# A bias prologue that stores its last blocks in two steps and divides the network's pieces anew

## The chip, the core and the metric

The kernel runs on one core of a Trainium2 chip. The metric is the device time of one execution in microseconds (us), and of several executions the median. The engines are named as the profile names them: PE (TensorE, matrix products; PEld is its weight load), DVE (VectorE), ACT (ScalarE), POOL (GpSimd) and SP (SyncE, which only issues DMA transfers here; ACT and POOL have queues for issuing them too).

## What is computed

Attention over 8 batches, 8 heads, 576 positions and head size 64, with a position bias that a small network makes, and behind it a gated network of three matrix products on all 4608 tokens:

```python
scores = scale * np.matmul(q, k.transpose(0, 1, 3, 2))
psi_rel = np.log1p(np.abs(pos[:, None] - pos[None, :]))
psi_i = np.log1p(np.maximum(pos[:, None], 1.0))
h = np.maximum((psi_rel / psi_i)[..., None] @ w1 + b1, 0.0)   # 32 hidden values per pair (i, j)
scores = scores + (h @ w2).transpose(2, 0, 1)[None]           # one bias per head, the same for every batch
attn = softmax(scores)
x = (attn @ v) with the heads side by side                    # 4608 x 512
out = ((x @ moe_w1) * (x @ moe_w2)) @ moe_w3 @ moe_w_out
```

The bias depends on the head and on the pair of positions (i, j) alone: for a row i it is a function of the distance |i - j|, scaled by a factor of the row. So it is computed once, ahead of the attention, and kept in DRAM.

## The kernel before, in words

**The prologue** (inside `with ExitStack() as pro`) makes the bias in 36 groups of 16 rows. A group has four *pieces* of the network: `hidden(grp)` computes relu of one piece for all distances that the group needs (304 to 576 columns), on DVE (`zdve`, 14 buffers, L534) or on ACT (`zact`, 6 buffers, L532). `bias_group(G)` then multiplies the four pieces by `w2` on PE into a `bacc` bank in PSUM (L549, four banks), and ACT evicts it twice, once forwards and once mirrored, into a tile `bev` of 128 partitions by 591 columns (L562). Partition 8 i + h of `bev` is row i of the group for head h. SP stores the tile into `nb_d` in DRAM (L564, 295.5 KB). The tile comes from the pool `ep`, which has four buffers, so the eviction of group G waits until the store of group G - 4 has landed. Which pieces ACT takes is chosen by a small planner with costs per column (`COST`, `who`).

**Loading the bias.** The attention works on units (p, b): a pair of heads p and a batch b, 32 units. For each unit nine tiles of scores are made: tiles 0 to 7 (rows 128 (t // 2) onwards of head t % 2 of the pair) and M (the last 64 rows of both heads). `load_bias(0, t, True)` fetches the bias tile `nb` of the first pair from `nb_d` (L270, L272, L273, on SP) when its last group is stored: tiles 6 and 7 need group 31, tile M group 35. The first unit needs heads 0 and 1 alone; the other six heads are wanted when the next pairs of heads begin, from unit 6 on.

**Units.** For a unit, S (L320, PE) makes scores of a tile, T (L331, DVE) adds the bias and takes the row's extreme, E (L356, ACT) makes the exponentials, F (L377 to L389, PE) transposes them, H (L400 on DVE, L402 on ACT) moves these out of PSUM into `PTX[u % 2]`, W (L434, PE) multiplies by `v`. `ORDER` gives each step a time within the unit; units follow each other every `PERIOD` = 12.31. The order of T is 0, 3, 1, 5, 6, 2, 7, M, 4. Ahead of S stand the splits of `k` and `q` into a high and a low part: for unit 0 on ACT (L300) and DVE (L301), for every later unit on POOL (gk and gq, L303 and L304). `raw` has one buffer for `k` and one for `q`, so the next unit's load (L287, SP) waits for the split of the one before. `ppM` tiles have zeros at their sides, which POOL clears after the prologue (L589).

**Order of the work.** Each step is put into a list with a due time (`put`, `plan.append`), and `drive` issues a list in the order of these times. There are separate lists for the prologue (all that is due before 0) and for the attention (`later`). DVE, ACT, PE and POOL keep to the order within a list, but a step of a later list may be put among those of an earlier one; SP's order is chosen by the framework. An engine runs its instructions in order, so one that waits holds all behind it. Group G is due at -48 + 1.25 G, with its pieces 0.7 before that, its products 1.0 and its eviction 2.5 after it.

**Memory.** The prologue's pools lie on a stack, in the order in which they are opened, and `ppool` (the exponentials), `pt` (the two `PTX` tiles) and `sm` take their place afterwards.

Of the kernel before, what the change touches and what calls it, by code (L numbers as in the profile page):

```python
# [9 lines left out]
F32 = mybir.dt.float32  # L10
# [7 lines left out]

P = 128

LEAD, PACE_B, BUSY_D, BUSY_A, LAG_B = 48.00, 1.25, 1.95, 4.50, 6.15

FIRST = {"ldk": -42.0, "ldq": -41.0, "ldv": -4.0, "gk": -20.0, "gq": -15.0}
AT_LOW = -4.80
AT_BIAS = -0.7, 1.0, 2.5

AT_FO, PACE_F = 2.00, 2.80
# [71 lines left out]
def relpos_attention_moe(  # L99
# [17 lines left out]
    nc = tc.nc  # L117
    NPAIR, B, _, S = k.shape
    D, H = P // 2, 2 * NPAIR
# [90 lines left out]
    def drive(plan):  # L210

        E_ = mybir.EngineType
        with tc.manual_schedule(engines={E_.PE, E_.Activation, E_.DVE, E_.Pool}):
            for _, _, step in sorted(plan, key=lambda e: e[:2]):
                step()

    def put(plan, steps, *times):

        def one():
            next(steps, None)  # L220
        for at in times:
            plan.append((at, len(plan), one))
# [8 lines left out]
    NB_L, NB_W = 16, S + 32  # L231
    nb_d = dram.tile([H, (S + 1) * NB_W], F32, name="nb_d")
# [17 lines left out]
    st = {u: {"P": [None] * 9} for u in range(NU)}  # L250
# [10 lines left out]
    def load_bias(p, t, first=False):  # L261
        nb = NB[p, t] if first else nbp.tile([P, S], F32, name="nb")
        NB[p, t] = nb
        heads = (0, 1) if t == "M" else (int(t) % 2,)
        for h in heads:
            o = nb[(lo, hi)[h]] if t == "M" else nb
            r0 = 512 if t == "M" else int(t) // 2 * P
            rows = nb_v[2 * p + h, r0:r0 + o.shape[0], :]
            if h == 0:
                nc.sync.dma_start(o, rows)  # L270
            else:
                nc.sync.dma_start(o[:, S - 512:S], rows[:, 0:512])  # L272
                nc.sync.dma_start(o[:, 0:S - 512], rows[:, 512:S])  # L273
# [185 lines left out]
    later = []  # L459
# [7 lines left out]
        later.append((at, len(later), step, n, u))  # L467
    t_s = max(e[0] for e in later if e[3][0] in "SE") + 0.5
    end = max(e[0] for e in later) + 0.5
    later = [e[:3] for e in later]  # L470

    plan = [e for e in later if e[0] < 0.0] + [(AT_LOW, len(later) + i, lambda n=n: st[0].pop("low" + n)()) for i, n in enumerate("kq")]
    later = [e for e in later if e[0] >= 0.0]


    with ExitStack() as pro:
        sb = pro.enter_context(tc.tile_pool(name="pro", bufs=1))
        zp = pro.enter_context(tc.tile_pool(name="zp", bufs=14))
        ep = pro.enter_context(tc.tile_pool(name="ep", bufs=4))
        psb = pro.enter_context(tc.tile_pool(name="psb", bufs=4, space=PSUM))  # L480

        GI = P // HID
        NG = S // GI
        GM = GI * H
        GV = P // GM
        NGRP = NG // GV
        GR = GV * GI

        w1c = sb.tile([P, 1], F32, name="w1c")
        b1c = sb.tile([P, 1], F32, name="b1c")
        w2b = sb.tile([P, GM], F32, name="w2b")
        tsh = sb.tile([P, S], F32, name="tsh")
        beta = sb.tile([P, NG], F32, name="beta")
        post = sb.tile([P, NGRP], F32, name="post")
        nc.scalar.dma_start(w1c, w1.rearrange("g c -> (g c)").rearrange("(p o) -> p o", o=1))
        nc.sync.dma_start(tsh, logs.broadcast_to([P, S]))
        nc.scalar.dma_start(b1c, b1.rearrange("(p o) -> p o", o=1))
        nc.sync.dma_start(beta, logi)  # L500
        nc.scalar.dma_start(w2b, w2)
        nc.sync.dma_start(post, ilogs)
        nc.vector.tensor_scalar(beta, beta, b1c, None, op0=ALU.mult)
        nc.vector.tensor_scalar(tsh, tsh, w1c, None, op0=ALU.mult)

        def reach(G):

            return (G + 1) * GR - 1, S - 1 - G * GR


        COST = {"dve": (0.06, 0.00066), "act": (0.2, 0.00081)}
        busy = dict(dve=BUSY_D, act=BUSY_A)
        who = {}

        def charge(e, n):
            busy[e] += COST[e][0] + COST[e][1] * n

        for G in range(NGRP):
            n = max(reach(G)) + 1
            for vv in range(GV):  # L520
                e = min(busy, key=lambda e: busy[e] + COST[e][0] + COST[e][1] * n)
                who[G * GV + vv] = e
                charge(e, n)
            for m in (reach(G)[1] + 1, reach(G)[0]):
                charge("act", m)

        def hidden(grp):
            n = max(reach(grp // GV)) + 1
            on = who[grp]
            z = zp.tile([P, S], F32, name=f"z{on}", bufs={"dve": 14, "act": 6}[on])  # L530
            if on == "act":
                nc.scalar.activation(z[:, 0:n], tsh[:, 0:n], AF.Relu, bias=beta[:, grp:grp + 1])  # L532
            else:
                nc.vector.tensor_scalar(  # L534
                    z[:, 0:n], tsh[:, 0:n], beta[:, grp:grp + 1], 0.0, op0=ALU.add, op1=ALU.max,
                )
            return z

        def bias_group(G):
            L, R = reach(G)  # L540
            n = max(L, R) + 1
            zs = [hidden(g) for g in range(G * GV, (G + 1) * GV)]
            yield
            accs = []
            for c in range(0, n, 512):
                m = min(n - c, 512)
                acc = psb.tile([P, 512], F32, name="bacc")
                for vv in range(GV):
                    nc.tensor.matmul(  # L549
                        acc[vv * GM:(vv + 1) * GM, 0:m], w2b, zs[vv][:, c:c + m], start=True, stop=True,  # L550
                    )
                accs.append(acc)
            yield

            ev = ep.tile([P, S + GR - 1], F32, name="bev")
            for c, acc in zip((0, 512), accs):
                for at, d, a, b in ((L, 1, 0, R + 1), (L, -1, 1, L + 1)):
                    a, b = max(a, c), min(b, c + 512)
                    if a < b:
                        o = ev[:, at + a:at + b] if d > 0 else ev[:, at - b + 1:at - a + 1]  # L560
                        x = acc[:, a - c:b - c]
                        nc.scalar.activation(o, x if d > 0 else x[:, ::-1], AF.Copy, scale=post[:, G:G + 1])  # L562
            r0 = G * GR * NB_W + 1
            nc.sync.dma_start(  # L564
                nb_d[:, r0:r0 + GR * (NB_W + 1)].rearrange("h (i w) -> i h w", i=GR)[:, :, 0:L + R + 1], ev,
            )


        for G in range(NGRP):
            at = -LEAD + G * PACE_B  # L570
            put(plan, bias_group(G), *(at + d for d in AT_BIAS))
            for t in TILES:
                if G == (NGRP - 1 if t == "M" else 8 * (int(t) // 2) + 7):
                    plan.append((at + AT_BIAS[-1] + LAG_B, len(plan), lambda t=t: load_bias(0, t, True)))
        drive(plan)


# [14 lines left out]
    later = [e for e in later if e[0] >= t_s]  # L592
# [251 lines left out]
    for i in range(2 * NF):  # L844
        at = t_o + i * PACE_F
        hf, t = divmod(i, NF)
# [7 lines left out]
    later = [e for e in later if e[0] > end]  # L854
# [4 lines left out]
    plan, t_f = [], t_o + 2 * NF * PACE_F  # L859
# [22 lines left out]
    for i in range(len(EARLY_W), 2 * NF):  # L882
        n, k = divmod(i - len(EARLY_W) + 1, len(FREE_W))
# [103 lines left out]
```

## Time and profile before

| what | us |
|---|---|
| median of three runs (lowest, highest) | 1103.02 (1101.92, 1104.57) |
| the profiled execution's own time | 1102.86 |
| its span, from the first instruction to the last | 1101.0 |
| PE, DVE, ACT, POOL busy | 1062.7, 846.4, 679.1, 283.8 |
| first eviction of the prologue begins, last one ends | 9.28, 61.44 |

A row of the timeline or of a group names the engine, the line of the kernel, the operation, and output and input by the program's names; in square brackets is the idle time of the engine just before and what ended it. "x4" is a count. In the chain of waits each piece is a start, a length and what it is. SPq rows are issues of DMA transfers, which aren't counted as work of an engine.

### The profile page before, as it was taken

What the parts mean: (1) busy time and instruction counts of PE and PEld (TensorE: products, weight loads), DVE (VectorE), ACT (ScalarE), POOL (GpSimd) and SP (SyncE); (2) the same over time, 40 slices, a digit from 0 to 9 for tenths busy, and PEclk for the clock granted to TensorE, in tenths of its full rate; (3) what the DMA queues carried; (4) which work ended last, traced back from release to release, by engine and by line L of the source; (5) the groups of instructions that cost most, each with busy time, mean ns of one, the idle gap of its engine ahead of it and who ended that gap; (6) DMA issues with size and microseconds to landing.
All of it is one profiled execution on the core that took longest, in us unless ns stands there. A gap on an engine that the chain in (4) does not pass through costs nothing.

```text
span 1101.0 us, 23555 instructions
## 1 busy us (share of the span) xinstructions
PE 1062.7 (97%) x9300; PEld 889.2 (81%) x9300; DVE 846.4 (77%) x1746; ACT 679.1 (62%) x1288; POOL 283.8 (26%) x214
## 2 busy tenths in 40 slices
PE   6769999999999999999999999999999999999998
PEld 3257777777777777767898899999999999999997
DVE  8948887888788888867777867776786786777664
ACT  6869998898898899854433543453453445346332
POOL 0046774776677567530000000000000000000000
PEclk9979999999999999999999999999999999999999
DMA  6974575558455655327322131031012103101001
GB/s 215 284 226 126 175 216 172 157 176 270 131 168 172 201 160 175 98 68 173 115 82 86 44 115 58 1 115 34 24 51 79 44 1 115 29 1 58 1 1 58
DMA packets 58157, 123.19 MB, mean 112 GB/s; under 512 B 9152, under 2 KB 19264, under 8 KB 58048
## 3 DMA queue, kind: packets, MB, share of 16 engines
q1 hardware_dynamic: 56464, 119.95, 34.7%
q10 hardware_dynamic: 1584, 1.75, 0.5%
q8 instruction: 73, 1.20, 0.5%
q14 instruction: 36, 0.29, 0.1%
HBM read 91.76 MB, written 29.92 MB: 111 GB/s over the span
## 4 chain that ended last, share of the span: by engine, by line
PE 82%; DVE 8%; ACT 5%; DMA 3%; issue 1%; ACTq 0%; SPq 0%; DVEq 0%
PE up L767 27%; PE o L823 15%; PE pst L434 14%; PE s L320 13%; PE pst L377 6%; PE wacc L652 4%; DMA nb_d<-bev 2%; PE bacc L549 1%; ACT bev L562 1%; DVE url L737 1%; DVE wmag L193 1%; DVE wu L204 1%; ACT pt L402 1%; DVE g L785 1%; ACT gh L791 1%
## 5 line engine op out<-in xcount | busy, mean ns | idle before, releaser
L331 DVE CUSTOM_DVE_ANT_0 ts<-s,nb 128x576 f32<-128x576 f32 x288 | 211.1, 756 | 59.8 <-PE s L320 26.4
L356 ACT ACTIVATE pp<-ts,mx 128x576 f32<-128x576 f32 x256 | 195.3, 766 | 17.8 <-DVE mx L331 17.8
L767 PE MATMUL up<-xch,urh 128*128 128x384 f32 x560 | 189.8, 339 | 0.0
L767 PE MATMUL up<-xcl,urh 128*128 128x384 f32 x560 | 189.5, 338 | 0.0
L767 PE MATMUL up<-xch,url 128*128 128x384 f32 x560 | 189.0, 337 | 0.0
L823 PE MATMUL o<-w3s,gh 128*128 128x512 f32 x576 | 180.6, 395 | 0.0
L434 PE MATMUL pst<-pt,rv 128*64 128x320 f32 (+1 forms) x1280 | 169.3, 411 | 1.3 <-ACT pt L402 1.3
L791 ACT ACTIVATE gh<-g 128x384 fp32r<-128x384 f32 x96 | 50.5, 526 | 174.7 <-DVE g L785 174.7
L402 ACT ACTIVATE pt<-pst 128x1024 f32<-128x1024 f32 x128 | 128.6, 1020 | 30.7 <-PE pst L377 30.5
L785 DVE TENSOR_TENSOR wos<-up,wos 128x384 f32<-128x384 f32 x120 | 66.9, 558 | 99.4 <-PE up L767 98.3
L434 PEld LDWEIGHTS pst<-pt,rv 128*64 128x64 f32 x1280 | 86.3, 137 | 62.4 <-issue 10.1
L782 ACT COPY wos<-up 128x384 f32<-128x384 f32 x136 | 65.0, 478 | 114.9 <-PE up L767 113.3
L320 PE MATMUL s<-kh,qh 64*128 64x288 f32 x640 | 116.7, 357 | 8.7 <-DVE mx L331 7.7
L823 PE MATMUL o<-w3s,gl 128*128 128x512 f32 x288 | 113.9, 396 | 0.0
L767 PEld LDWEIGHTS up<-xch,urh 128*128 128x128 f32 x560 | 105.3, 188 | 9.2
L767 PEld LDWEIGHTS up<-xch,url 128*128 128x128 f32 x560 | 105.2, 188 | 9.1
L823 PEld LDWEIGHTS o<-w3s,gh 128*128 128x128 f32 x576 | 105.3, 188 | 5.5
L377 PE MATMUL pst<-ident,pp 64*128 64x64 f32 x2304 | 103.2, 225 | 2.3 <-ACT pp L356 1.3
L767 PEld LDWEIGHTS up<-xcl,urh 128*128 128x128 f32 x560 | 105.1, 188 | 0.0
L377 PEld LDWEIGHTS pst<-ident,pp 64*128 64x128 f32 x2304 | 99.9, 140 | 5.2 <-ACT pt L402 2.3
L400 DVE COPY pt<-pst 64x64 f32<-64x64 f32 (+3 forms) x160 | 82.1, 514 | 26.0 <-PE pst L434 24.2
L320 PE MATMUL s<-kh,ql 64*128 64x288 f32 x640 | 97.3, 295 | 0.0
(107 smaller groups left out, 1985.7 us busy)
## 6 DMA issues: line engine op xcount, KB each, us to landing
rq<-in_q_dram SPq DMA_DIRECT2D x31, 640.0 KB
wi<-in_moe_w_dram SPq DMA_DIRECT2D x32, 512.0 KB
nb_d<-bev SPq DMA_DIRECT2D x36, 295.5 KB
rv<-in_v_dram SPq DMA_DIRECT2D x32, 320.0 KB
x_d<-pt SPq DMA_DIRECT2D x32, 288.0 KB
xr<-x_d SPq DMA_DIRECT2D x24, 384.0 KB
rk<-in_k_dram SPq DMA_DIRECT2D x31, 288.0 KB
rb<-r_d SPq DMA_DIRECT2D x44, 192.0 KB
```

The costliest lines, as they stand in the source:

```text
L320: nc.tensor.matmul(s[:, hf, :HS], Q[x][rows, q0:q0 + P], K[y][rows, h * HS:(h + 1) * HS], start=(m == 0), stop=(m == len(ops) - 1),)
L331: nc.vector.tensor_tensor_reduce(out=halves(ts), in0=d.pop(("s", t))[:, :, :HS], in1=halves(NB[p, t]), op0=ALU.add, op1=ALU.min, scale=-1. ...
L356: nc.scalar.activation(pp, ts, AF.Exp, bias=mx, scale=-1.0, accum_out=sums[p][:, 9 * b + col:9 * b + col + 1])
L377: nc.tensor.transpose(ps[0:n, hf, c0:c0 + 64], x[rows], ident[rows, rows])
L400: nc.vector.tensor_copy(o, x)
L402: nc.scalar.activation(o, x, AF.Copy)
L434: nc.tensor.matmul(o, x[:, c0:c0 + D], m, start=(c == 0), stop=(c == 4))
L767: nc.tensor.matmul(acc, l[:, b, ks], r[:, k], start=(m == 0 and which in ("P1", "P2", "P5")), stop=(m == 3 * KH - 1), skip_group_check=whi ...
L782: nc.scalar.copy(d[name], d[src])
L785: nc.vector.tensor_tensor(o, a, b, op=op)
L791: nc.scalar.activation(d["gh"][:, i * CH:(i + 1) * CH], d["g"][:, i], AF.Copy)
L823: nc.tensor.matmul(d["o", t], l[:, sl], folded[ft][r], start=(ft == 0 and m == 0), stop=(ft == NF - 1 and m == 2),)
```

## The change

The last eight groups (`LATE_G` = 28 and up) store in two steps. SP first stores heads 0 and 1 alone, in two transfers of 16 partitions each; when the prologue's list reaches `AT_REST`, POOL's queue stores the whole tile, heads 0 and 1 again among it. These groups have a pool of their own, `eq`, with eight buffers; the other groups' pool `ep` has five in place of four, and is opened ahead of `zp`. The loads of bias tiles 6, 7 and M are due 3.00 after the last eviction that they need, in place of 6.15. The planner is replaced by a rule: ACT takes two pieces in each of groups 0 to 2, one in two groups of three from 3 to 27, none from 28 on. The POOL splits of unit 1 (gk and gq) go into the prologue's list, where they stand ahead of the whole stores.

```diff
--- before.py
+++ after.py
@@ -18,10 +18,11 @@
 P = 128
-LEAD, PACE_B, BUSY_D, BUSY_A, LAG_B = 48.00, 1.25, 1.95, 4.50, 6.15
+LEAD, PACE_B, LAG_B, LAG_L = 48.00, 1.25, 6.15, 3.00
 FIRST = {"ldk": -42.0, "ldq": -41.0, "ldv": -4.0, "gk": -20.0, "gq": -15.0}
 AT_LOW = -4.80
+LATE_G, AT_REST = 28, 6.00
 AT_BIAS = -0.7, 1.0, 2.5
 AT_FO, PACE_F = 2.00, 2.80
@@ -467,16 +468,17 @@
         later.append((at, len(later), step, n, u))
     t_s = max(e[0] for e in later if e[3][0] in "SE") + 0.5
     end = max(e[0] for e in later) + 0.5
-    later = [e[:3] for e in later]
-    plan = [e for e in later if e[0] < 0.0] + [(AT_LOW, len(later) + i, lambda n=n: st[0].pop("low" + n)()) for i, n in enumerate("kq")]
-    later = [e for e in later if e[0] >= 0.0]
+    first = [("gk", 1), ("gq", 1)]
+    plan = [e[:3] for e in later if e[0] < 0.0 or e[3:] in first] + [(AT_LOW, len(later) + i, lambda n=n: st[0].pop("low" + n)()) for i, n in enumerate("kq")]
+    later = [e[:3] for e in later if e[0] >= 0.0 and e[3:] not in first]
     with ExitStack() as pro:
         sb = pro.enter_context(tc.tile_pool(name="pro", bufs=1))
+        ep = pro.enter_context(tc.tile_pool(name="ep", bufs=5))
         zp = pro.enter_context(tc.tile_pool(name="zp", bufs=14))
-        ep = pro.enter_context(tc.tile_pool(name="ep", bufs=4))
+        eq = pro.enter_context(tc.tile_pool(name="eq", bufs=8))
         psb = pro.enter_context(tc.tile_pool(name="psb", bufs=4, space=PSUM))
         GI = P // HID
@@ -508,25 +510,13 @@
             return (G + 1) * GR - 1, S - 1 - G * GR
-        COST = {"dve": (0.06, 0.00066), "act": (0.2, 0.00081)}
-        busy = dict(dve=BUSY_D, act=BUSY_A)
-        who = {}
-        def charge(e, n):
-            busy[e] += COST[e][0] + COST[e][1] * n
-        for G in range(NGRP):
-            n = max(reach(G)) + 1
-            for vv in range(GV):
-                e = min(busy, key=lambda e: busy[e] + COST[e][0] + COST[e][1] * n)
-                who[G * GV + vv] = e
-                charge(e, n)
-            for m in (reach(G)[1] + 1, reach(G)[0]):
-                charge("act", m)
+        def on_act(G):
+            return 2 if G < 3 else 0 if G >= LATE_G else int(G % 3 < 2)
         def hidden(grp):
             n = max(reach(grp // GV)) + 1
-            on = who[grp]
+            on = "act" if grp % GV < on_act(grp // GV) else "dve"
             z = zp.tile([P, S], F32, name=f"z{on}", bufs={"dve": 14, "act": 6}[on])
             if on == "act":
                 nc.scalar.activation(z[:, 0:n], tsh[:, 0:n], AF.Relu, bias=beta[:, grp:grp + 1])
@@ -552,7 +542,7 @@
                 accs.append(acc)
             yield
-            ev = ep.tile([P, S + GR - 1], F32, name="bev")
+            ev = (ep if G < LATE_G else eq).tile([P, S + GR - 1], F32, name="bev")
             for c, acc in zip((0, 512), accs):
                 for at, d, a, b in ((L, 1, 0, R + 1), (L, -1, 1, L + 1)):
                     a, b = max(a, c), min(b, c + 512)
@@ -561,17 +551,22 @@
                         x = acc[:, a - c:b - c]
                         nc.scalar.activation(o, x if d > 0 else x[:, ::-1], AF.Copy, scale=post[:, G:G + 1])
             r0 = G * GR * NB_W + 1
-            nc.sync.dma_start(
-                nb_d[:, r0:r0 + GR * (NB_W + 1)].rearrange("h (i w) -> i h w", i=GR)[:, :, 0:L + R + 1], ev,
-            )
+            o = nb_d[:, r0:r0 + GR * (NB_W + 1)].rearrange("h (i w) -> i h w", i=GR)[:, :, 0:L + R + 1]
+            if G < LATE_G:
+                nc.sync.dma_start(o, ev)
+            else:
+                for h in range(2):
+                    nc.sync.dma_start(o[:, h], ev[h:P:H])
+                yield
+                nc.gpsimd.dma_start(o, ev)
         for G in range(NGRP):
             at = -LEAD + G * PACE_B
-            put(plan, bias_group(G), *(at + d for d in AT_BIAS))
+            put(plan, bias_group(G), *(at + d for d in AT_BIAS), *((AT_REST + 0.1 * G,) if G >= LATE_G else ()))
             for t in TILES:
                 if G == (NGRP - 1 if t == "M" else 8 * (int(t) // 2) + 7):
-                    plan.append((at + AT_BIAS[-1] + LAG_B, len(plan), lambda t=t: load_bias(0, t, True)))
+                    plan.append((at + AT_BIAS[-1] + (LAG_B if G < LATE_G else LAG_L), len(plan), lambda t=t: load_bias(0, t, True)))
         drive(plan)
```

## The prediction

> **What bounds the kernel now.** I began with the table of windows, to see from where on TensorE never waits.
>
> ```profile
> core 0: us, PE busy (x) PEld busy (x) DVE busy (x) ACT busy (x) POOL busy (x), PEclk, DMA share, GB/s
> 9.28:61.45 52.17, 40.14 (x369) 15.92 (x361) 46.64 (x128) 42.62 (x99) 2.09 (x2) 1.00 0.84 263
> 49.70:61.45 11.75, 9.80 (x104) 4.31 (x104) 8.29 (x18) 9.49 (x24) 2.09 (x2) 1.00 0.96 301
> 61.45:67.80 6.35, 0.64 (x6) 0.41 (x6) 0.82 (x3) 1.64 (x5) 4.27 (x6) 0.62 0.77 249
> 86.30:98.85 12.55, 12.55 (x189) 9.64 (x186) 10.21 (x28) 11.62 (x24) 8.38 (x8) 1.00 0.45 138
> 111.40:460.00 348.60, 347.57 (x5010) 265.43 (x5007) 290.83 (x725) 310.34 (x628) 237.12 (x171) 1.00 0.56 176
> ```
>
> Columns: stretch, its length, then busy time and count of PE, PEld, DVE, ACT and POOL, then granted clock, DMA share, GB/s. From 86.30 on PE is busy 12.55 of 12.55 us, later 347.57 of 348.60: whatever moves PE's work at 86.30 moves the end by as much. Ahead of it PE does nearly nothing from 61.45 to 67.80 (0.64 of 6.35), and then runs at a lower clock (0.62 here). In the bias prologue (9.28 to 61.45) ACT is the fullest after DVE, 42.62 of 52.17, and at its end the DMA engines are full: 0.96, 301 GB/s. So next, the chain of waits around the hole, and the table of waits up to 100 us.
>
> ```profile
> 34.32 3.18 DMA nb_d<-bev
> 48.13 4.52 DMA nb_d<-bev
> 61.46 0.52 SPq L564
> 62.07 0.54 SPq L270
> 62.66 4.81 DMA nb<-nb_d
> 67.80 2.53 PE s L320 x18
> ```
>
> ```profile
> ACT bev L562 <- DMA nb_d<-bev: 6.2, 9, 1.6
> DVE ts L331 <- DMA nb<-nb_d: 5.6, 1, 5.6
> ```
>
> The last store goes out, SP then issues the loads of bias tiles 6 and 7, and T6, the fifth softmax step of unit 0, waits 5.6 us for them. Before that ACT lost 6.2 us in nine waits for one of the four `bev` buffers, each behind a store of 3.2 to 4.5 us (3.18 and 4.52 above). The timeline gives the instants:
>
> ```profile
> 9.28 0.85 ACT L562 ACTIVATE bev<-bacc,post 128x512 f32<-128x512 f32 x2 [3.07 <-PE bacc L549]
> 5.47 24.74 DVE L534 TENSOR_SCALAR zdve<-tsh,beta 128x576 f32<-128x576 f32 x70
> 54.18 0.90 ACT L562 ACTIVATE bev<-bacc,post 128x80 f32<-128x80 f32 x2
> 60.38 1.06 ACT L562 ACTIVATE bev<-bacc,post 128x16 f32<-128x16 f32 x3 [1.56 <-DMA nb_d<-bev]
> 55.11 0.53 SPq L564 DMA_DIRECT2D nb_d<-bev  x1
> 52.86 0.75 DVE L301 TENSOR_TENSOR kl<-rk,kh 128x576 fp32r<-128x576 f32 x1
> 53.53 1.49 DVE L301 TENSOR_TENSOR ql<-rq,qh 128x1280 fp32r<-128x1280 f32 x1
> 55.94 0.76 DVE L331 CUSTOM_DVE_ANT_0 ts<-s,nb 128x576 f32<-128x576 f32 x1 [0.93 <-PE s L320]
> 66.98 0.76 DVE L331 CUSTOM_DVE_ANT_0 ts<-s,nb 128x576 f32<-128x576 f32 x1 [5.61 <-DMA nb<-nb_d]
> ```
>
> Group 31's eviction (the 128x80 row) ends at 55.08 and its store is issued at 55.11; the last eviction, group 35, waits 1.56 us for a buffer and ends at 61.44. DVE finishes its pieces of the network at 52.86, then splits `k` and `q` (to 55.02). T0 starts at 55.94, T6 at 66.98.
>
> **The change part by part.** *Pieces of the network.* The prices:
>
> ```profile
> L331 DVE CUSTOM_DVE_ANT_0 ts<-s,nb 128x576 f32<-128x576 f32 x288 | 211.1, 756 | 59.8 <-PE s L320 26.4
> L562 ACT ACTIVATE bev<-bacc,post 128x512 f32<-128x512 f32 (+34 forms) x80 | 33.1, 495 | 12.6 <-DMA nb_d<-bev 6.2 <-PE bacc L549 6.2
> L532 ACT ACTIVATE zact<-tsh,beta 128x496 f32<-128x496 f32 (+13 forms) x17 | 11.7, 689 | 0.0
> L534 DVE TENSOR_SCALAR zdve<-tsh,beta 128x576 f32<-128x576 f32 (+17 forms) x126 | 45.4, 449 | 2.1 <-PE bacc L549 2.0
> ```
>
> ACT goes from 18 to 23 pieces of 144, by the old planner's arithmetic against the new rule: 6 in groups 0 to 2 (before 1), 17 in groups 3 to 27 (before 12), none from 28 on (before 5). DVE gets 121 instead of 126. Its pieces cost 45.4/126 = 0.36 us each; five long early ones and five of middle length leave it and five long late ones come, so 43.5 in place of 45.4: from 5.47 they end at 49.0 if never held, and at 51 if the 2 us of holds of now (52.86 - 5.47 - 45.4) stay. I take 50.2; the splits (2.16) end at 52.4, T0 follows at 52.9, and T6, four steps of 0.76 us and some waits for TensorE later, could run at 56.7. The six early pieces on ACT end at 5.47 + 6 x 0.69 = 9.6, where its first eviction started at 9.28: 0.3 late, since it idled there.
>
> *Five buffers, then eight of their own.* From its first eviction ACT needs 42.6 us of work; its later pieces are as many (17) and a little shorter (-1). With no wait for buffers it ends group 35 at 9.6 + 41.6 = 51.3, and group 31 four evictions (about 4 us) earlier, at 47.3; with half of the 9.5 us of waits of now, at 52. I take 48.5 for group 31.
>
> *Two heads first.* Eight stores of 295.5 KB are replaced on SP by 16 of an eighth of that, 37 KB each.
>
> ```profile
> L564 SPq DMA_DIRECT2D nb_d<-bev x36: 517/524/1228, 10.4 to 61.5; - x36
> ```
>
> SP pays 0.52 us an issue, so 1.04 a group, about ACT's own pace: nothing lies behind it but loads. In the critical stretch 8 x 295.5 - 16 x 36.9 = 1774 KB (1.8 MB) are gone, 6 us of full DMA at 301 GB/s. No row shows the landing of a store this small: between 2 us (half of the quickest whole store) and 4.52; I take 4, since whole stores of groups 23 to 27 stand in the same queues. By the Trainium skill (DMA: Bandwidth & Descriptors, Anatomy of one DMA — SWDGE path) a DMA costs about 2.0 us and its bytes at 436 GB/s, an estimate of 2.1 us here, by which T6 could be up to 1.9 us earlier; its rule (Rules for kernel authors) that transfers under 64 KB are mostly overhead speaks against cutting a store in pieces. No row here shows either. The loads of tiles 6 and 7 then go out at 48.5 + 1.0 + 4 = 53.5 and land after 0.54 + 4 (now 0.54 + 4.3): 58. So T6 starts at 56.7 to 58, I take 57.3: 9.7 us earlier. Bounds 55 and 60.
>
> *Next late: GpSimd.* Here lies the price of the change.
>
> ```profile
> 45.79 0.40 PE L320 MATMUL s<-kh,qh 64*128 64x288 f32 x2 [0.76 <-ACT qh L300]
> 84.72 1.91 ACT L402 ACTIVATE pt<-pst 128x1024 f32<-128x1024 f32 x2
> 63.85 1.26 POOL L303 TENSOR_SCALAR qh<-rq 128x1280 fp32r<-128x1280 f32 x1 [1.95 <-DMA rq<-in_q_dram]
> 65.19 2.89 POOL L304 TENSOR_TENSOR ql<-rq,qh 128x1280 fp32r<-128x1280 f32 x1
> 71.87 0.67 POOL L303 TENSOR_SCALAR kh<-rk 128x576 fp32r<-128x576 f32 x1 [3.79 <-PE s L320]
> 75.35 2.92 POOL L304 TENSOR_TENSOR ql<-rq,qh 128x1280 fp32r<-128x1280 f32 x1
> 61.49 0.41 POOL L589 MEMSET ppM<- 128x64 f32 x4 [1.08 <-ACT bev L562]
> 72.62 0.59 PE L320 MATMUL s<-kh,qh 64*128 64x288 f32 x2
> 57.32 0.54 SPq L287 DMA_DIRECT2D rq<-in_q_dram  x1
> 86.30 0.38 PE L320 MATMUL s<-kh,qh 64*128 64x288 f32 x2
> ```
>
> Unit 1's `q` is loaded once the split of unit 0's has freed its buffer (issue 57.32, use 63.85, 6.5 us), and GpSimd's last piece of unit 1 ends at 68.08, 4.5 us ahead of S0 of unit 1 (72.62). Now the split ends at 52.4, the load goes out at 53.5 and takes 5.2 with fewer stores beside it, and gq of unit 1 ends after 4.3 us more at 63.0: S0 of unit 1, due at 72.62 - 9.7 = 62.9, just gets it. Putting gk and gq of unit 1 into the prologue's plan keeps them ahead of the stores. But the eight whole stores stand next on GpSimd. They overwrite what tiles 6, 7 and M read, so they wait for these loads (58, and some 60 for M, hidden behind gq, which ends at 63). Behind them stand gk and gq of unit 2, 71.87 to 78.27, so 6.4 us, possibly the four clears of `ppM` (0.4 us), and then S0 of unit 2, which is at 86.30 now with 8 us of slack.
>
> No DMA is issued by GpSimd in this trace. A store there costs no less than SP's 0.52 us, and at most GpSimd's longest instruction, 2.92. I take 1.2, the nearest row that isn't SP's quick case: the longest issue of this very store on SP (1.228). By the Trainium skill (same page, SWDGE vs HWDGE vs iDMA and the latency table) the path from GpSimd has a program write its descriptors and takes about 1 us to the first byte; with 1.0 the sum below gives 1094.2.
>
> Unit 2's `q` is then ready at 63.0 + 8 x 1.2 + 0.4 + 6.4 = 79.4, needed 0.2 us after S0's start. S0 of unit 2 stands at 79.2, 7.1 us earlier than 86.30. With 0.52 GpSimd is done at 74.0 and the 9.7 us of T6 hold; with 2.92 it is done at 93.2 and the kernel loses 6.7. The break-even is (86.5 - 69.8)/8 = 2.1 us a store.
>
> *Without price.* `eq` lies behind `zp`, so under the second `PTX` tile, whose first write is H0 of unit 1 (84.72 now, 77 then); the last store is issued at 72.6 and has left `eq` by 77. If that cover fails ACT waits by the lateness. The stores' bytes move to where DMA has room (0.77 from 61.45, 0.45 from 86.30).
>
> **Sum.** The profiled execution took 1102.86 us (span 1101.0 and 1.86 around it); 1102.86 - 7.1 = 1095.8. The median of the runs, 1103.02, differs by 0.16 only, so 1095.8 it is.
>
> **Rivals.**
> *A. GpSimd doesn't decide* (a store costs under 0.9 us, or gk of unit 2 is put ahead of the stores): all of T6's 9.7 us arrive, and, PE's clock being kept, about 1 us more (S0 of unit 2 stands 19.3 us after T6 now, 18.35 in the order as written): 1092 to 1093. For it: ready instructions overtake here (S0's first product runs at 45.79 among the bias products). Against: the stores are ready when gq ends.
> *B. The load is late anyway.* DMA is full: groups 3 to 27 come faster (one whole store per 1.2 us of ACT is 250 GB/s, and `k`, `q` and six bias tiles beside them, 2.7 MB in 34 us, make it 330, over the 301 of the fullest stretch), so a backlog stands ahead of the small stores. Each us of it beyond my 4 lands on T6; with 5 us T6 gains 4.7 and the time is 1098. Against: 6 us of DMA are taken out, and five stores may be on their way.
> *C. Slower.* A store on GpSimd costs over 2.1 us: S0 of unit 2 is later than 86.5 and PE waits in order; at 2.5 us it is 3.3 us late, 1106. For it: POOL's 128-partition operations take 1.26 to 2.92 us. Against: a store touches no data on GpSimd. The Trainium skill (SBUF — State Buffer, Who interferes with whom) says that DVE in its two-port mode keeps GpSimd from writing descriptors; the pieces of the network are such instructions, but they are over 10 us before the stores, so by it C gets no more.
> *D. No change:* the store costs 2.1, or order changes eat the gain. 1102.5.
>
> **Numbers.** Forecast 0.55, A 0.15, B 0.14, C 0.11, D 0.05. The forecast's own range, stores of 1.0 to 1.6 us, is 1094 to 1099; the range that holds the time 8 times in 10 takes in most of A and B, 1091 to 1100.5. What this measurement tells from no change is 0.2%, 2.2 us. Faster: forecast, A and nearly all of B, 0.83; same: D and a rest of B, 0.06; slower: C, 0.11.
>
> **What would show it.** In the profile after: ACT's waits for `bev` buffers under 2 us; evictions over by 54; T6 at 55 to 60 with a wait for `nb` under 2 us; GpSimd's eight stores between 60 and 75, about 1.2 us apart; S0 of unit 2 near 79, held by `ql`; PE full from there. The prediction is wrong if T6 comes after 61, if the stores cost under 0.9 or over 1.8 us each, or if S0 of unit 2 waits for something else.

## The result, and the profile after

The changed kernel is slower: 1114.78 us (median of four runs, 1113.53 to 1115.66) against 1103.23 (1101.92 to 1104.57), a ratio of 1.0114 with a 95% interval of 1.01 to 1.0128. The forecast was 1095.8 with a range to 1100.5: wrong in sign.

The profiled execution of after took 1115.66 us, span 1113.8: 12.8 more than that of before. First the sums of its page: did any engine get more work?

```profile
PE 1061.1 (95%) x9300; PEld 887.0 (80%) x9300; DVE 844.9 (76%) x1741; ACT 681.0 (61%) x1293; POOL 288.7 (26%) x222
```

None did: PE is busy for 1061.1 us, 1.6 less than before. So a gap must have opened, and the table of windows of TensorE shows it (stretch, length, PE's busy time and count, granted clock, DMA share, GB/s):

```profile
50.00:55.00 5.00, 4.42 (x45) 1.00 0.33 103
...
70.00:75.00 5.00, 0.67 (x6) 0.68 0.99 320
75.00:80.00 5.00, 2.23 (x16) 0.50 0.97 363
80.00:85.00 5.00, 0.00 (x0) 0.50 0.44 153
```

From 70 to 85 us PE works 2.90 of 15 us, and what it does then runs at 0.50 to 0.68 of the clock. The timeline of VectorE (T0, T6, tile M's step and, behind the gap, a step of unit 1), ScalarE, GpSimd and PE:

```profile
49.73 3.48 DVE L524 TENSOR_SCALAR zdve<-tsh,beta 128x560 f32<-128x560 f32 x8
54.34 1.06 ACT L552 ACTIVATE bev<-bacc,post 128x16 f32<-128x16 f32 x3 [0.66 <-PE bacc L539]
55.90 0.76 DVE L332 CUSTOM_DVE_ANT_0 ts<-s,nb 128x576 f32<-128x576 f32 x1 [0.63 <-PE s L321]
...
64.28 0.76 DVE L332 CUSTOM_DVE_ANT_0 ts<-s,nb 128x576 f32<-128x576 f32 x1 [5.40 <-DMA nb<-nb_d]
...
73.42 0.76 DVE L332 CUSTOM_DVE_ANT_0 ts<-s,nb 128x576 f32<-128x576 f32 x1 [6.33 <-DMA nb<-nb_d]
...
73.70 2.14 POOL L561 DMA_DIRECT2D nb_d<-bev  x4 [2.64 <-DMA nb<-nb_d]
...
82.86 1.94 ACT L403 ACTIVATE pt<-pst 128x1024 f32<-128x1024 f32 x2 [14.63 <-issue]
85.58 0.76 DVE L332 CUSTOM_DVE_ANT_0 ts<-s,nb 128x576 f32<-128x576 f32 x1 [9.24 <-ACT pp L357]
...
97.15 0.38 PE L321 MATMUL s<-kh,qh 64*128 64x288 f32 x2
```

And the view of line 561, the whole stores:

```profile
L561 POOL DMA_DIRECT2D nb_d<-bev x8: 530/532/714, 66.0 to 75.3; - x8
...
who waited for it (us, times):
  ACT pt L403: 14.6, 1
...
DMA to landing us min/median/max: 3.6/6.6/8.8
```

The 82.86 row is H0 of unit 0, the first write into `PTX`. ACT was free at 68.23 and sat idle for 14.63 us. The row itself names no releaser ("issue" stands for time in which the profile shows none); the view of the stores does: what waited for them is "ACT pt L403", 14.6 us. ACT runs in order, so the exponentials behind H0 stand too, and with them T (9.24 us at 85.58, "ACT pp") and S. The 97.15 row is 10.85 us later than its counterpart in before (86.30). The prediction calls that row S0 of unit 2, but it is S3, the step behind it: a unit has ten such rows (one for each tile, two for M), and this is the 22nd. S0 itself went from 84.75 to 95.61, so the delay is the same. How much of it arrives at the end shows in the store of a unit's result, `x_d`, whose first and last issue stand in one row of that tensor's view. Before:

```profile
L443 SPq DMA_DIRECT2D x_d<-pt x32: 319/327/1267, 95.8 to 498.3; - x32
```

After:

```profile
L444 SPq DMA_DIRECT2D x_d<-pt x32: 319/327/538, 106.6 to 511.0; - x32
```

The first unit is done 10.8 us later (106.6 against 95.8), the last 12.7 (511.0 against 498.3), the span is 12.8 longer. So most of the loss is in the start, and 1.9 us more are lost between the first unit and the last.

### The profile page after: what moved, and what is told of

It reads as the page before. It is cut to its first block, busy times and chain, and to the rows that moved or that the text cites. A ratio compares the mean times of both kernels' runs of the same rounds, so it can differ in the third digit from the quotient of the medians.

```text
span 1113.8 us, 23596 instructions
## 1 busy us (share of the span) xinstructions
PE 1061.1 (95%) x9300; PEld 887.0 (80%) x9300; DVE 844.9 (76%) x1741; ACT 681.0 (61%) x1293; POOL 288.7 (26%) x222
## 4 chain that ended last, share of the span: by engine, by line
PE 80%; DVE 9%; ACT 6%; issue 3%; DMA 2%; SPq 0%; POOL 0%; ACTq 0%; DVEq 0%; POOLq 0%
PE up L762 27%; PE o L818 15%; PE pst L435 14%; PE s L321 12%; PE pst L378 6%; PE wacc L647 4%; DMA nb_d<-bev 1%; ACT bev L552 1%; DVE wmag L194 1%; ACT pp L357 1%; DVE url L732 1%; ACT pt L403 1%; DVE wu L205 1%; ACT zact L522 1%; DVE zdve L524 1%
## 5 line engine op out<-in xcount | busy, mean ns | idle before, releaser
L403 ACT ACTIVATE pt<-pst 128x1024 f32<-128x1024 f32 x128 | 128.6, 1021 | 44.5 <-PE pst L378 29.7
```

What stands on the lines that cost most here:

```text
L403: nc.scalar.activation(o, x, AF.Copy)
```

## The experiments

The theory: H0 waits not for what lies under the tile that it writes but for what lies under the whole pool `pt`, from which both `PTX` tiles come. `eq` lies under the second tile only (by the program's allocation it takes bytes 122784 to 141724 of a partition; the first tile is 99520 to 122560, the second 122560 to 145600), so the prediction let only H0 of unit 1 wait. The rivals: the two steps of storing cost the time in another way (queues, DMA traffic), or the new division does.

### Two pools for PTX

```diff
-    pt = att.enter_context(tc.tile_pool(name="pt", bufs=1))
+    pt = [att.enter_context(tc.tile_pool(name=f"pt{i}", bufs=1)) for i in range(2)]
...
-    PTX = [pt.tile([P, 9, SQW], F32, name=f"pt{i}") for i in range(2)]
+    PTX = [pt[i].tile([P, 9, SQW], F32, name=f"pt{i}") for i in range(2)]
```

> The changed kernel, but the two PTX tiles come from two pools in place of one; they keep their places in memory, and eq lies under the second alone. Theory (the first H step of unit 0 waits for GpSimd's whole stores because the pool of both PTX tiles opens as one over eq): that wait of 14.6 us goes, H0 of unit 0 starts within 1 us of its transposes (near 70), and the time falls by 9 to 11 us to 1104 to 1106, not under 1103, because tile M's load still lands 3 us later than before the change (TM at 73.4 against 70.5). Rival (H0 waits for something else that comes as late, such as tile M or ql of unit 2): the time stays within 3 us of the changed kernel's 1114.8.

Measured: 1102.35 us against 1102.27 for before on the same chip, ratio 1.0 [0.9986, 1.0014]. The timeline of ScalarE, VectorE, GpSimd and PE:

```profile
55.05 0.76 DVE L332 CUSTOM_DVE_ANT_0 ts<-s,nb 128x576 f32<-128x576 f32 x1 [0.63 <-PE s L321]
...
62.19 0.76 DVE L332 CUSTOM_DVE_ANT_0 ts<-s,nb 128x576 f32<-128x576 f32 x1 [4.17 <-DMA nb<-nb_d]
...
66.44 1.97 ACT L403 ACTIVATE pt<-pst 128x1024 f32<-128x1024 f32 x2 [0.29 <-PE pst L378]
...
68.67 0.76 DVE L332 CUSTOM_DVE_ANT_0 ts<-s,nb 128x576 f32<-128x576 f32 x1 [3.66 <-ACT pt L403]
69.35 2.13 POOL L561 DMA_DIRECT2D nb_d<-bev  x4
...
72.86 2.92 POOL L305 TENSOR_TENSOR ql<-rq,qh 128x1280 fp32r<-128x1280 f32 x1
...
80.61 0.38 PE L321 MATMUL s<-kh,qh 64*128 64x288 f32 x2
...
82.17 0.38 PE L321 MATMUL s<-kh,qh 64*128 64x288 f32 x2
```

The last two rows are S0 and S3 of unit 2. The view of `x_d`:

```profile
L444 SPq DMA_DIRECT2D x_d<-pt x32: 319/327/1199, 91.6 to 495.7; - x32
```

The wait is gone: H0 starts at 66.44 after 0.29 us, before the last four of GpSimd's stores are even issued (69.35). The slowdown of 0.0114 is gone whole, and more than I had expected: tile M's step comes at 68.67, 1.8 us ahead of before (70.47), where I had it 3 us behind. The tiles kept their places in memory and nothing else was touched, so the wait was the pool's. GpSimd, which the prediction took for the next limit, is done with unit 2's `q` at 75.78 (the 72.86 row), 4.8 us ahead of S0 of unit 2 at 80.61. It is no gain over before, though.

### The same two pools in the other places

```diff
-    pt = [att.enter_context(tc.tile_pool(name=f"pt{i}", bufs=1)) for i in range(2)]
+    pt = [att.enter_context(tc.tile_pool(name=f"pt{i}", bufs=1)) for i in (1, 0)][::-1]
```

> The two PTX tiles stay in pools of their own, but change places in memory: pt0, which unit 0 writes first, now covers the eight buffers of the late groups. If the wait of H0 of unit 0 comes from what lies under the tile's own pool (my theory), it comes back: some 10 to 14 us at the first pt eviction, until the eighth of GpSimd's stores has landed, and the time is 1112 to 1117 us. If it came from something that two pools change in another way (their number, the order of the plan), it stays away, and the time is 1100 to 1104, as with the places as they were.

Measured: 1113.33 us, ratio 1.0092 [1.0067, 1.0116]. The timeline of ScalarE and GpSimd:

```profile
73.36 2.13 POOL L561 DMA_DIRECT2D nb_d<-bev  x4 [1.74 <-DMA nb<-nb_d]
...
82.56 1.94 ACT L403 ACTIVATE pt<-pst 128x1024 f32<-128x1024 f32 x2 [14.03 <-issue]
```

The wait is back with 14.03 us, with two pools and the same order of work. So it is the place that decides: in this program the first write into a pool waits for the transfers that read what lay under it.

### Four groups instead of eight

The changed kernel with its one pool; groups 28 to 31 go out whole from SP, 32 to 35 in two steps (the division as in the change).

```diff
-LATE_G, AT_REST = 28, 6.00
+LATE_G, AT_REST = 32, 6.00
...
-            return 2 if G < 3 else 0 if G >= LATE_G else int(G % 3 < 2)
+            return 2 if G < 3 else 0 if G >= 28 else int(G % 3 < 2)
```

> The changed kernel with its one pool, but only groups 32 to 35 stored twice; groups 28 to 31 are stored whole from SP's queue at once. If the first pt eviction waits for the last landing of any store under the pool, four stores fewer change little: the last four were issued at 73.7 to 75.8 us and set the end of the wait at 82.9, so H0 starts at 78 to 83 and the time is 1109 to 1115. If the wait were a matter of how many stores GpSimd issues, half of them would halve it: 1107 to 1109.

Measured: 1107.9 us, ratio 1.0049 [1.0032, 1.0066]. The timeline of GpSimd and ScalarE:

```profile
65.34 2.30 POOL L561 DMA_DIRECT2D nb_d<-bev  x4 [1.23 <-DMA nb<-nb_d]
...
75.69 1.94 ACT L403 ACTIVATE pt<-pst 128x1024 f32<-128x1024 f32 x2 [10.01 <-issue]
```

Both my numbers for H0 (78 to 83) were missed, and the time fell where the rival had put it, though not for the rival's reason. The four stores that are left are not issued at 73.7, as I had supposed: with four fewer ahead of them they follow the split of `q` at once, at 65.34, 8.4 us earlier than the last four of after. H0 starts 7.2 us earlier (75.69 against 82.86), and the ratio is 0.65% lower, 7.2 us. So the end of the wait follows the last store's landing. It comes 7.0 us after the last issue in after (73.70 + 2.14 = 75.84 to 82.86), 7.1 in the kernel with places exchanged (75.49 to 82.56), 8.1 here (67.64 to 75.69). In the trace of after the last packets of GpSimd's queue fall between 81 and 82 us, just ahead of 82.86.

### No whole stores

Two heads first, but no whole stores behind; the tiles 6, 7 and M of the later pairs of heads read other rows in their place, so heads 2 to 7 lack their own bias in the last 192 rows.

```diff
+            r0 = 0 if p and (t == "M" or int(t) > 5) else r0
...
-                nc.gpsimd.dma_start(o, ev)
```

> The changed kernel without GpSimd's eight whole stores, so heads 2 to 7 get no bias for the last 128 rows; the loads of these tiles for the later pairs read the first rows instead, with the same bytes. Theory: both costs of the whole stores go, the wait of H0 of unit 0 and the traffic beside tile M's load. T6 stays near 64.3, TM comes by 70.5, and the time is 1099 to 1102, 2 to 4 us under the kernel before. If the traffic isn't what makes tile M late, TM stays near 73 and the time is 1104 to 1106, as with two pools.

Measured: 1100.44 us, ratio 0.9985 [0.9974, 0.9996], as forecast. The timeline of VectorE, T6 and tile M's step:

```profile
63.20 0.76 DVE L333 CUSTOM_DVE_ANT_0 ts<-s,nb 128x576 f32<-128x576 f32 x1 [4.33 <-DMA nb<-nb_d]
...
68.53 0.76 DVE L333 CUSTOM_DVE_ANT_0 ts<-s,nb 128x576 f32<-128x576 f32 x1 [2.51 <-ACT pt L404]
```

With the wait gone, everything else that the eight stores cost (GpSimd's time, 2.4 MB of traffic, queue order) is a difference of 0.0015 to the two pools, and the intervals overlap. Tile M's step comes when it came with two pools (68.67). The two-pool version still has all of the stores and their traffic, so queue and traffic are out as the cause of the 11.6 us.

### The new division alone

```diff
-        COST = {"dve": (0.06, 0.00066), "act": (0.2, 0.00081)}
...
-                who[G * GV + vv] = e
+        def on_act(G):
+            return 2 if G < 3 else 0 if G >= 28 else int(G % 3 < 2)
```

> The kernel before with the new division of the pieces alone; stores, pools and loads as before. Theory (the prologue's end is set by the stores and by SP's queue rather than by ACT or DVE): the evictions end at 58 to 62, T6 at 65 to 68, time 1101 to 1104, no change that can be told. Rival (the division alone brings ACT's gain): last eviction by 56, T6 by 62, time under 1099.

Measured: 1104.48 us, ratio 1.0021 [1.001, 1.0032]. I had expected no change (1101 to 1104); it is a little slower. DVE, which now has all late pieces, is held for `zdve` buffers that PE has not read yet, 7.1 us in all up to 60 us (2.0 in before), and T0 comes at 59.89 where it was at 55.94. The timeline of VectorE:

```profile
48.37 8.82 DVE L521 TENSOR_SCALAR zdve<-tsh,beta 128x496 f32<-128x496 f32 x21 [2.57 <-PE bacc L536]
...
59.89 0.76 DVE L331 CUSTOM_DVE_ANT_0 ts<-s,nb 128x576 f32<-128x576 f32 x1 [0.63 <-PE s L320]
...
68.02 0.76 DVE L331 CUSTOM_DVE_ANT_0 ts<-s,nb 128x576 f32<-128x576 f32 x1 [5.16 <-DMA nb<-nb_d]
```

The view of `x_d`:

```profile
L443 SPq DMA_DIRECT2D x_d<-pt x32: 319/327/1250, 95.4 to 498.3; - x32
```

T6 is only 1.0 us later than in before (68.02 against 66.98), because it waits for its load anyway (5.16 us). In this profile (1103.04 us) the delay is gone by the first `x_d` store, 95.4 against 95.8, and the last is at 498.3 in both. So the 2 us of the median are not explained by the late T0; where they arise is not shown.

### The old division with two pools

The planner of before in the two-pool version.

> Two pools for PTX, and the division of the network's pieces as it was before; of the change only the two ways of storing are left. If the new division costs time by itself (it measured 1104.5 against 1102.3 on the kernel before), this is 1 to 2 us below the 1102.35 of the two pools with the new division: 1100 to 1101.5. If the division is needed so that the last groups are evicted early, T6 comes after 63 us instead of 62.2 and the time is 1102 to 1104.

Measured: 1101.76 us, ratio 0.9997 [0.9984, 1.001]; T6 at 62.76 in the timeline, 0.6 later than with the new division, and a time between the two forecasts. It does not tell them apart: with eight buffers for the late groups the division makes no difference that can be measured.

### Where the other queue stands

In after, SP's queue holds back the first rows. Its timeline, with the ScalarE row of the evictions of groups 28 to 31 ahead of it:

```profile
45.55 3.42 ACT L552 ACTIVATE bev<-bacc,post 128x128 f32<-128x128 f32 x8
48.23 3.42 SPq L559 DMA_DIRECT2D nb_d<-bev  x5
53.90 0.35 SPq L288 DMA_DIRECT2D rk<-in_k_dram  x1
54.30 3.01 SPq L559 DMA_DIRECT2D nb_d<-bev  x5
...
59.22 0.53 SPq L271 DMA_DIRECT2D nb<-nb_d  x1
```

The tables of waits, SP's from 45 to 70 us and ScalarE's up to 56:

```profile
SPq L288 <- DVE kl L302: 2.2, 1, 2.2
...
ACT bev L552 <- DMA nb_d<-bev: 2.5, 3, 1.7
```

The ACT row (two evictions for each group) ends at 48.97, so group 31 is evicted then. Its two small stores are the seventh and eighth in the order as written. After five of them the load of unit 1's `k` stands in the queue; it waits 2.2 us for DVE's split, and the eleven others stand behind it. The load of tile 6 goes out at 59.22, right behind the store before it, so it is the queue that it waited for. So in the two-pool version `k` and `q` of unit 1 were loaded from GpSimd's queue:

```diff
-        queue = nc.scalar if u == 0 and which != "v" else nc.sync
+        queue = nc.scalar if u == 0 and which != "v" else nc.gpsimd if u == 1 and which != "v" else nc.sync
```

> The changed kernel with two PTX pools, and the loads of k and q of unit 1 issued on GpSimd's queue in place of SP's. Theory (T6 is late in the changed kernel because SP stands still for 2.2 us in the load of k, and issues 16 small stores behind it): SP's small stores run without that hole, T6 starts at 59 to 61 in place of 64.3, and the time is 1100 to 1103. Rival (the DMA engines, not SP's queue, make tile 6 late): T6 stays at 63 to 65 and the time is that of two pools alone within 1 us.

Measured: 1101.11 us, ratio 0.9991 [0.9977, 1.0004]. The timeline of SP, VectorE and ScalarE:

```profile
48.23 8.47 SPq L559 DMA_DIRECT2D nb_d<-bev  x12
56.80 0.53 SPq L271 DMA_DIRECT2D nb<-nb_d  x1
...
61.68 0.76 DVE L332 CUSTOM_DVE_ANT_0 ts<-s,nb 128x576 f32<-128x576 f32 x1 [3.21 <-DMA nb<-nb_d]
...
79.87 1.94 ACT L403 ACTIVATE pt<-pst 128x1024 f32<-128x1024 f32 x2 [1.65 <-DMA nb_d<-bev]
```

The time is as expected, T6 not: 61.68, where 59 to 61 was forecast. The twelve small stores run without a gap now, but at 0.71 us each and with four of groups 32 and 33 among them, so the load of tile 6 still goes out at 56.80. The last row shows the wait that the prediction had looked for: the first write into the second tile, which does lie over `eq`, 1.65 us late.

The same edit on the kernel before:

> The kernel before with one edit: k and q of unit 1 are loaded from GpSimd's queue instead of SP's. Nothing of the storing changes. Theory: SP's queue gives up two issues of 0.54 us each, T6 moves by 1 us at most and the time is 1101 to 1103, no change that can be told. The rival, that this move alone gave the gain of the version with groups 28 to 31 stored whole (0.997), makes it 1098.5 to 1100.5.

Measured: 1104.03 us, ratio 1.0013 [1.0004, 1.0022], 1 us above the range that I had given. T6 moved by 3.1 us (63.84), not by 1 at most, but tile M's step stayed (70.36 against 70.47). There is no gain by itself.

### Four groups, two pools

The edits of three kernels together: two pools, four groups in two steps, `k` and `q` of unit 1 on GpSimd's queue.

> Two pools, k and q of unit 1 loaded from GpSimd's queue, and only groups 32 to 35 stored twice (28 to 31 whole from SP, the division as in the change). Against the same with eight groups (1101.1, T6 61.7, a wait of 1.6 us at the first eviction into the second PTX tile) four of GpSimd's stores fall away, so that wait goes, and tile M's load shares the DMA with 1.2 MB less; T6 waits for whole stores instead of first rows, 1 to 3 us more. Theory: the start is worth little, since the clock takes a part of a lead back later: 1099.5 to 1102. The rival, that all of a lead of the start arrives at the end, gives 1097 to 1099.

Measured: 1099.88 us, ratio 0.997 [0.9956, 0.9984], within the forecast. Once more, unchanged:

> The version that measured 0.997 [0.9956, 0.9984], once more and unchanged, to see whether it holds. If it does: a ratio of 0.996 to 0.9985, with the first pt eviction at 68 us and the first x_d store at 92. If the earlier figure was luck, the ratio is above 0.9985.

Measured: 1100.0 us, ratio 0.997 [0.996, 0.998]: it holds. And with the loads of `k` and `q` back on SP's queue:

> Two pools, k and q of unit 1 back on SP's queue, and only groups 32 to 35 stored twice. If the gain of that version came from storing groups 28 to 31 once, it stays here: 1099.5 to 1101. If it needed the loads on GpSimd's queue as well, this is 1101 to 1102.5, as with eight groups and the loads on SP (1102.35).

Measured: 1098.37 us (1096.14 to 1101.01), ratio 0.9966 [0.9952, 0.9979]. The time is under the range that I had given, and the loads on GpSimd's queue aren't needed. This version, the change with two pools for `PTX` and only the last four groups in two steps, is 0.3% faster than the kernel before. Its timeline:

```profile
57.45 0.76 DVE L332 CUSTOM_DVE_ANT_0 ts<-s,nb 128x576 f32<-128x576 f32 x1 [0.63 <-PE s L321]
...
64.11 0.76 DVE L332 CUSTOM_DVE_ANT_0 ts<-s,nb 128x576 f32<-128x576 f32 x1 [3.69 <-DMA nb<-nb_d]
...
67.60 0.76 DVE L332 CUSTOM_DVE_ANT_0 ts<-s,nb 128x576 f32<-128x576 f32 x1 [0.67 <-PE s L321]
```

The view of `x_d`:

```profile
L444 SPq DMA_DIRECT2D x_d<-pt x32: 320/327/1398, 92.9 to 495.9; - x32
```

The VectorE rows are T0, T6 and tile M's step. This execution reached T0 2.4 us later than the one with eight groups (57.45 against 55.05; with four groups and one pool it was 55.04), and still T6 follows T0 after 6.66 us instead of 7.14, and tile M's step follows T6 after 3.49 us instead of 6.48. With eight groups, then, 3 us of T6's lead were lost again at tile M (in the kernel before the two steps are 3.49 apart). SP has four issues fewer and GpSimd four stores fewer. GpSimd's stores are not needed for the loss: without any of them the two steps are still 5.33 apart (63.20 and 68.53 above). Whether it is SP's queue was not tried by itself; the rows at 68.67 and 68.53 name ACT's H step, which this step of VectorE doesn't use. Nor does the profile show where the 0.3% come from: it is of the slowest of the six executions (1101.01), and its last `x_d` store is no earlier than with eight groups (495.9 against 495.7).

### Where a lead goes

In the two-pool version the first unit is done 4.2 us ahead of before (91.6 against 95.8), the last only 2.6 (495.7 against 498.3), and over all runs the medians are equal. These are the windows of TensorE at the change from attention to the network, the only place between 100 and 1090 us where any of the 13 profiles has a clock under 1.00. Before:

```profile
470.00:480.00 10.00, 9.92 (x75) 1.00 0.23 80
480.00:490.00 10.00, 7.93 (x58) 1.00 0.19 58
```

The change with two pools:

```profile
470.00:480.00 10.00, 7.93 (x41) 0.96 0.25 84
480.00:490.00 10.00, 10.00 (x61) 0.87 0.17 55
```

The last version, two pools and four groups:

```profile
470.00:480.00 10.00, 9.12 (x47) 1.00 0.24 84
480.00:490.00 10.00, 8.81 (x60) 1.00 0.17 55
```

Every version has a gap of about 2.1 us in PE here. Behind it the two-pool version's clock is granted at 0.96 and 0.87: 10 x 0.04 + 10 x 0.13 = 1.7 us of clock, and 1.6 us of the lead are gone. Before and the last version have no such dip in their profiles, and from the first `x_d` store to the last they take 402.5 and 403.0 us, against 404.1. After has it too (0.83 from 490 to 500, 404.4). It is the same over all 13: the eight with a dip take 403.9 to 404.4 us from the first `x_d` store to the last, the five without 402.5 to 403.0. Whether the dip comes is not tied to the start: the kernel before with the loads moved shows it as well (0.83 from 480 to 490), with the first store at 94.5. So a lead of a few microseconds is in part lost or kept by the clock. What brings the dip, and why the two-pool version's median is 1.9 us above its profiled run, no run here settled.

## Why the prediction was wrong

**The step that failed** is the one without price: "`eq` lies behind `zp`, so under the second `PTX` tile, whose first write is H0 of unit 1". The place was right. But the write that waits is the first into the pool, and that is H0 of unit 0, 14.6 us too early for the stores. Shown from both sides: two pools take the wait away (1102.35), the same two with places exchanged bring it back (1113.33), and its end moves with the last store's landing (1107.9). The text had the clause "if that cover fails ACT waits by the lateness" but gave it no place in the range: it asked when `eq` is free, not who asks first. No rival had it; C, the slower one, was about GpSimd's price.

**Two heads first, T6 at 57.3: failed too.** It came at 64.28, 2.7 us ahead of before and not 9.7. Group 31 was evicted when I said (48.5 forecast, about 49 measured, and ACT waited 2.5 us for buffers where "under 2" stood). What I left out is SP's order: six small stores belong ahead of group 31's, and a load that waits stood among them. "Nothing lies behind it but loads" was looking the wrong way; a load lay in front. Even without the pool's wait the forecast would thus have missed: two pools measure 1102.35, not 1095.8. In their profile T6 is at 62.19, 4.9 us later than forecast, 3 us are lost at tile M, and the row at 86.30 in before has come forward to 82.17, by 4.1 us and not by 7.1.

**A row misread.** The 86.30 row from which the sum starts is S3 of unit 2; S0, which needs GpSimd's `ql`, stands at 84.75. GpSimd's slack was thus 6.7 us and not 8, the break-even 1.9 us a store and not 2.1, and S0 at 79.2 would have been a gain of 5.5 us, 1097.3 in place of 1095.8. The sign stays the same, and so does the step that failed.

**GpSimd's price: mis-sized.** A whole store there costs 0.53 us (eight at 0.530 to 0.714), not 1.2: SP's own price, the lower bound. So rival A's condition held, and C's and D's did not, but A's gain of T6 didn't exist. What counted was the landing, 6.6 us in the median, while the DMA engines moved up to 363 GB/s. By the Trainium skill (DMA: Bandwidth & Descriptors, Anatomy of one DMA — SWDGE path), 2.0 us and the bytes at 436 GB/s, it would be 2.7 us, an estimate; the quickest of the eight took 3.6, so the trace doesn't agree for stores in a full queue.

**The pieces of the network: late by 3 us.** DVE's pieces ended at 53.2 in place of 50.2, T0 came at 55.90, not 52.9. In another execution of the same prologue (two pools) T0 was at 55.05, so about 1 us of it is spread. The evictions, which were to be over by 54, ended at 55.4.

**Rival B** (the load is late anyway, 1098) had the right kind of mistake, lateness on T6, but put it down to a backlog of DMA. Between 50 and 55 us, where it was to be, the trace of after has a DMA share of 0.33 (0.92 in the 5 us before): the transfers weren't late, their issue was.

## What to carry to other kernels

Where a buffer of an earlier stage is still being read by a late transfer, find the first write into anything allocated over it, and count the whole pool, not the tile: that write is the due time of the last landing. Before a transfer is moved, list the queue that issues it in order, with the wait of each entry ahead of it, since a single waiting load delays all that follow it. A gain in the start counts at the end only as far as nothing in between, the clock included, takes it back.

## What had not been expected of the hardware

An issue on GpSimd's queue costs as little as on SP's, 0.53 us for 128 rows of 2.4 KB, and the same store takes 3.6 to 8.8 us to land. A store of 37 KB costs SP no less to issue than one of 295 KB: a median of 0.54 us over the sixteen of after, against 0.52 for the whole stores of before; in a row the small ones go out every 0.60 to 0.71 us. After a gap of 2.1 us in a stretch that is otherwise full, TensorE's granted clock dipped in eight of the 13 profiles (0.83 to 0.90 over 10 us) and not in the other five, and the dip is worth about 1.5 us of 1100. Over the 35 runs of before on one chip a clock lower by 0.001 goes with a time 0.5 us longer; over 22 runs on another chip it is 0.1.
